# Coarse attention of two steps together on eight array tiles, with TensorE's order written out

## The chip, the cores and the metric

The kernel runs on one core of a Trainium2 chip (trn2). The metric is device time in microseconds (us) of one execution, the median over runs. TensorE is written PE, VectorE DVE, ScalarE ACT, GpSimd POOL, and SP is the engine that starts most transfers.

## The reference

Eight batches of eight heads, 576 positions, head dimension 64. Each head has two attentions, summed; a gated convolution over the 512 channels of a batch follows.

```
q_d, k_d, v_d = means of q, k, v over 4 neighbours        # 144 coarse positions
out_d   = softmax(scale * q_d @ k_d.T) @ v_d               # coarse attention
out_up  = repeat(out_d, 4)
scores  = where(|i - j| < 4, scale * q @ k.T, -1e9)        # local attention
x       = out_up + softmax(scores) @ v                     # then heads to channels
gate    = sigmoid(sum over 5 taps of conv_w[k] * x shifted by k)
out     = (gate * (x @ w_val)) @ w_out                     # float32 throughout
```

## The kernel before

A step is two pairs of heads of a batch, four heads; there are 16 steps (`NSTEP`), two to a batch. The kernel records each piece of work as an operation with its engine, a duration, what it needs and what it must wait for (`op`), and a planner (`Planner`) then plays all operations through and writes each engine's instructions in the order that comes out. PE's order is the one that the planner is given as a list: `tensor_order` makes it from `FIRST`, `PACE` and `TURN`. `SHIFT` moves due times, which decide among ready operations on DVE, ACT and POOL. For some operations the planner also picks the engine (`either`). Nothing is reordered on the chip: each engine runs its list and waits.

A step i has these operations. `sla`, `slb` (line 722): local scores in two halves, 24 matmuls each and 4 that add the band mask. `mx`, `sub`, `exp`, `sum`, `rcp`, `norm`, `turn`, `spr`: their softmax, a 32x32-block transpose on DVE and four copies. `sd` (line 811): coarse scores, 20 matmuls of 144 columns, five for each of four q (q is a head of the step); the result stands on 32 partitions for each q. Each coarse matmul of steps 4 to 15 reads 64 rows and fills 32 columns of the array (a 64x32 tile; steps 0 to 3 sum over 128 rows); the four q's lie on four of its eight such tiles. `cmx0`, `cbi`, `cexp`, `cgrd`, `crcp`, `cnorm`, `cturn`: the coarse softmax, with one buffer `pd` for the probabilities and one, `pdt`, for their transpose. `odp` (line 932): coarse values, 20 matmuls on tiles of 32 rows and 64 columns, again four of eight. `oc` (line 945): ACT copies them to `od`. `xa`, `xb` (line 888): local values in two halves of 24 matmuls on 64x64 tiles, written into free columns of the PSUM tiles that `odp` opened. `xu`, `xt` (line 903): DVE adds local and repeated coarse values into `xt`, in four instructions of 288 columns.

The convolution of a pair p: `xh`, `xl` split `xt` into two fp32r parts (POOL, ACT or DVE), `tap4` and four `tap`s on DVE (line 994) form the gate's argument in a buffer `gp`, ACT applies tanh. A block j of 504 (at the end 288) positions runs through two projections: `v` (val, lines 1096 to 1098: three fp32r matmuls for each of four channel chunks), `h` on DVE (gate times value), its split `hhi`, `hlo`, then `o` (out, the same three lines) and its copy and store. In PE's list, `p` counts such matmul groups.

PSUM has eight banks: three tiles of two banks under the tag "a" (`AB`), shared by local scores, coarse scores and the values of a step, and two tiles of one bank for the projections. Before, `odp` takes two of the three "a" tiles and they come free with the step's last `xt`. In the first stretch some matmuls on constants (line 579) keep PE busy.

SP starts the loads of `qk` (two for each pair), `vw` (local values), the first quarter of `qs` and `vs` (batches' four-neighbour sums, whose other three quarters POOL adds by accumulating transfers, line 606), the weights and the stores. The planner allows eight SP transfers at a time (`OUTSTANDING`).

## Time and profile before

| | us |
|---|---|
| median of 3 runs (367.65 to 465.03) | 369.12 |
| profiled execution | 368.75 |
| its span, first to last instruction | 367.0 |
| PE busy / DVE busy / ACT busy / POOL busy | 341.5 / 309.0 / 208.3 / 158.2 |
| share of PE in the chain that ended last | 62% |

One run of the three, 465.03, stands far from the other two. The span is what the trace shows; 1.75 us of the execution lie outside it. Busy time on PE counts overlapping matmuls once, and a matmul's end is modelled, so the distance from one start to the next says more than a duration. A float32 matmul appears as two records. "Idle before, <- X" names what ended a wait.

### The profile page before, as it was taken

How to read it: one execution, taken by the hardware profiler on the slowest of the kernel's cores; microseconds unless marked ns; L12 is line 12 of the kernel's file. 1: busy time of each engine (PE TensorE's matmuls, PEld its weight loads, DVE VectorE, ACT ScalarE, POOL GpSimd, SP SyncE). 2: the span in 40 equal slices, each digit the busy share in tenths (PEclk: the TensorE clock that was granted, in tenths of full speed). 3: DMA queues.
4: the chain of work that ended last, by engine and by line, in shares of the span. 5: the costliest groups of instructions: out<-in, count | busy, mean ns of one | idle time of the engine just before them, and what ended most of it. 6: DMA issues, size and time to landing. Idle time of an engine off the chain costs nothing.

```text
span 367.0 us, 12798 instructions
## 1 busy us (share of the span) xinstructions
PE 341.5 (93%) x5500; PEld 268.2 (73%) x5500; DVE 309.0 (84%) x487; ACT 208.3 (57%) x530; POOL 158.2 (43%) x170
## 2 busy tenths in 40 slices
PE   8669669699999999999999999999799999999996
PEld 5546447577787777777777777777577778788996
DVE  4699989999899999999999998999988993836720
ACT  1388556746676865587555756675376465314421
POOL 6878732955504644434453245633582323001100
PEclk9998889899999999999999999999999999999999
DMA  7999499899897799887989997969523301102012
GB/s 229 352 362 349 113 292 293 226 199 178 272 305 173 234 267 293 234 210 223 293 205 224 274 248 195 220 183 308 140 49 113 116 3 63 51 2 86 28 50 80
DMA packets 23464, 70.95 MB, mean 193 GB/s; under 512 B 3184, under 2 KB 9584, under 8 KB 23408
## 3 DMA queue, kind: packets, MB, share of 16 engines
q1 hardware_dynamic: 17504, 52.39, 41.0%
q0 software_dynamic: 5616, 17.50, 26.5%
q8 instruction: 43, 0.70, 0.7%
q10 hardware_dynamic: 288, 0.26, 0.2%
q14 instruction: 13, 0.11, 0.1%
HBM read 60.69 MB, written 9.44 MB: 191 GB/s over the span
## 4 chain that ended last, share of the span: by engine, by line
PE 62%; DVE 20%; ACT 7%; DMA 4%; issue 3%; SPq 1%; POOL 1%; ACTq 0%; POOLq 0%; DVEq 0%
PE out L1096 8%; PE val L1096 7%; PE out L1097 7%; PE out L1098 7%; DVE gp L994 7%; PE val L1098 6%; PE val L1097 6%; PE x L888 6%; PE x L932 4%; DMA qk<-in_qk 4%; PE sd L811 4%; PE sl L722 2%; DVE xt L903 2%; ACT pd L855 2%; ACT pt L574 2%
## 5 line engine op out<-in xcount | busy, mean ns | idle before, releaser
L994 DVE SCALAR_TENSOR_TENSOR gp<-xt,cw,gp 128x576 f32<-128x576 f32 x128 | 111.4, 902 | 1.3 <-ACT gp L979 0.6
L1096 PE MATMUL val<-xhs,wh_v 128*128 128x504 f32 (+1 forms) x160 | 64.0, 400 | 0.0
L1098 PE MATMUL val<-xls,wh_v 128*128 128x504 f32 (+1 forms) x160 | 60.3, 377 | 0.3 <-POOL xls L969 0.3
L1097 PE MATMUL val<-xhs,wl_v 128*128 128x504 f32 (+1 forms) x160 | 60.0, 375 | 0.0
L1096 PE MATMUL out<-hhl,wh_o 128*128 128x504 f32 (+1 forms) x144 | 58.6, 407 | 0.5 <-DVE h L1124 0.4
L1098 PE MATMUL out<-hhl,wh_o 128*128 128x504 f32 (+1 forms) x144 | 54.7, 380 | 0.0
L1097 PE MATMUL out<-hhl,wl_o 128*128 128x504 f32 (+1 forms) x144 | 54.6, 379 | 0.0
L1005 ACT ACTIVATE gp<-gp 128x576 f32<-128x576 f32 x32 | 21.9, 685 | 28.1 <-DVE gp L994 27.9
L1186 ACT ACTIVATE ob<-out 128x504 f32<-128x504 f32 (+2 forms) x40 | 21.8, 554 | 27.8 <-PE out L1098 24.0
L888 PEld LDWEIGHTS x<-pt,vw 64*64 64x64 f32 x1536 | 26.4, 138 | 14.6 <-issue 6.4
L903 DVE TENSOR_TENSOR xt<-x,od 128x288 f32<-128x288 f32 x64 | 26.0, 441 | 13.0 <-PE x L888 13.0
L1096 PEld LDWEIGHTS val<-xhs,wh_v 128*128 128x128 f32 x160 | 30.3, 190 | 8.5 <-issue 2.9
L1144 POOL TENSOR_TENSOR hhl<-h,hhl 128x504 fp32r<-128x504 f32 (+2 forms) x24 | 26.8, 1148 | 19.7 <-ACT hhl L574 19.1
L1098 PEld LDWEIGHTS val<-xls,wh_v 128*128 128x128 f32 x160 | 30.4, 190 | 5.9 <-POOL xls L969 0.7
L1096 PEld LDWEIGHTS out<-hhl,wh_o 128*128 128x128 f32 x144 | 27.0, 188 | 9.0 <-issue 3.3
L574 POOL COPY pt<-pt 32x576 f32<-32x576 f32 x23 | 16.9, 733 | 38.6 <-PE x L888 29.7
L1097 PEld LDWEIGHTS val<-xhs,wl_v 128*128 128x128 f32 x160 | 30.4, 190 | 4.1
L888 PE MATMUL x<-pt,vw 64*64 64x48 f32 x1536 | 30.1, 225 | 3.3 <-DVE xt L903 2.4
L606 POOL DMA_DIRECT2D vs<-in_vgr x21 | 20.3, 968 | 29.0 <-DMA vs<-in_vgr 20.8
L855 ACT ACTIVATE pd<-pd,crs 128x144 f32<-128x144 f32 x75 | 24.6, 405 | 12.3 <-DVE crs L849 12.2
L722 PE MATMUL sl<-qk 128*24 128x60 f32 x1536 | 26.8, 215 | 4.7 <-issue 2.0
L831 ACT ACTIVATE pd<-sd,cbi 128x144 f32<-128x144 f32 x80 | 29.9, 386 | 2.1 <-DVE h L1124 1.6
(94 smaller groups left out, 675.8 us busy)
## 6 DMA issues: line engine op xcount, KB each, us to landing
qk<-in_qk SPq DMA_DIRECT2D x64, 291.0 KB, 7.3
vw<-in_vw SPq DMA_DIRECT2D x16, 768.0 KB, 6.0
qs<-in_qkr POOLq DMA_DIRECT2D x18, 576.0 KB, 8.2
out_t<-ob SPq DMA_DIRECT2D x32, 252.0 KB, 4.6
vs<-in_vgr POOLq DMA_DIRECT2D x21, 320.0 KB, 7.5
qs<-in_qkr SPq DMA_DIRECT2D x6, 576.0 KB, 10.5
vs<-in_vgr SPq DMA_DIRECT2D x7, 320.0 KB, 7.2
raw_v<-in_w_val SPq DMA_DIRECT2D x4, 512.0 KB, 8.2
```

The lines of the kernel that those rows point to most:

```text
L574: (nc.scalar.copy if eng is nc.scalar else eng.tensor_copy)(out=to, in_=of)
L722: nc.tensor.matmul(out=sc[32 * q : 32 * q + BQ, 2 * KW * g : 2 * KW * (g + 1)].rearrange("p (h k) -> p h k", h=2), lhsT=t[:, 1, 3 + blk : ...
L831: nc.scalar.activation(out=pd[:, g, 0:SD], in_=s["cs"][:, g], func=AF.Exp, scale=1.0 / 128.0, bias=s["bi"][:, g : g + 1], accum_out=s["csm ...
L855: nc.scalar.mul(w[:, g], w[:, g], s["crs"][:, g : g + 1])
L888: nc.tensor.matmul(out=s["x", pr][r, part, 0:HALF].rearrange("p (e g j) -> p e g j", e=2, j=BQ)[:, :, g], lhsT=s["vw"][(LO, HI)[pr], n + h ...
L903: nc.vector.tensor_tensor(out=xt, in0=s["x", pr][:, part, 0:HALF].rearrange("p (e j r) -> p e j r", e=2, r=FAC), in1=od.broadcast_to([P, 2 ...
L994: nc.vector.scalar_tensor_tensor(out=s["gp"], in0=s["xt"][:, k : k + S], scalar=cw[:, c, k : k + 1], in1=s["gp"], op0=ALU.mult, op1=ALU.add,)
L1005: nc.scalar.activation(out=s["gp"], in_=s["gp"], func=AF.Tanh, scale=0.5)
L1096: nc.tensor.matmul(out=o, lhsT=wh[:, d, col], rhs=his[d], start=d == 0, stop=False)
L1097: nc.tensor.matmul(out=o, lhsT=wl[:, d, col], rhs=his[d], start=False, stop=False)
L1098: nc.tensor.matmul(out=o, lhsT=wh[:, d, col], rhs=los[d], start=False, stop=d == NC - 1)
L1144: eng.tensor_tensor(out=t["hl"][:, cs], in0=t["h"][:, cs], in1=t["hh"][:, cs].bitcast(F32), op=ALU.subtract)
```

## The change

From step 4 on, the two steps of a batch are computed together in the coarse attention. One call of `sd` computes the first three of five groups of queries for both steps (24 matmuls), a second call the other two (16); one call of `odp` computes the values of both steps (40 matmuls), two PSUM tiles, one for each step. In the odd step the two heads of a pair are exchanged (`^ n % 2`, and the host lays out `vg` accordingly), so that both steps' matmuls lie on different tiles of the array. The probabilities and their transposes share three buffers (`pds`); guard and reciprocal run once for a pair of steps. `xa` and `xb` each have a PSUM tile of their own, freed by one DVE add over both pairs (576 columns); the coarse values are copied by one ACT instruction for a step and their tiles are then free. There are two double `xt` buffers instead of four single ones and six `gp` buffers instead of seven.

PE's order is one list (`FIRST`), without `PACE`, `HOLD` and `TURN`. `SHIFT` grows from 17 to some 700 words. SP starts a transfer only when at most 3,000,000 bytes were started after the last one known to have landed (`FLIGHT`; `paced`, and a dependency between the two transfers). The planner's own costs for code loading change, which alters no instruction by itself. The first loads are put in a slightly different order (`EARLY`).

```diff
-GB = 7
+GB = 6
...
-PACE = ((2, 10), (4, 29), (14, 189))
-HOLD = 6
 OPENING, SWITCH = 33000, 200
...
-TURN = (("sla slb", 1, 3), ("sd", 1, 3), ("odp", 0, 3), ("xa", 0, 3), ("xb", 0, 4))
-    "l0 sd0 l1 sd1 odp0 x0 p2 odp1 p4 l2 p2 x1 sd2 p2"
+    "sla0 sd0 sd1 sla1 xb0 slb0 xa0 slb1 odp0 p4 odp1 p1 xb1 xa1 p3 sla2 sd2 sd3 sla3 odp2 p8 xa2 xb2 sd4 p7 odp3 xa3 sd5 xb3 sla4 slb2 p9 slb4 odp4 xa4 "
...
-CODE, FETCH, BEAR = 256, 5500, 300
+CODE, FETCH, BEAR = 256, 2700, 300
+FLIGHT = 3000000
...
+        def paced(now):
+
+            kept, left = [], FLIGHT
+            for x in reversed(sent):
+                left -= ops[x]["size"]
+                if left < 0:
+                    if x not in end or end[x] > now:
+                        return False
+                    kept = [x]
+                    break
+            self.behind = kept
...
-    pd = cpool.tile([P, NG, 32 * NB], F32, name="pd")
+    pds = [cpool.tile([P, NG * 32 * NB], F32, name=f"pd{i}") for i in range(3)]
-    xts = [cpool.tile([P, 4 + S], F32, name=f"xt{i}") for i in range(4)]
+    xts = [cpool.tile([P, 2, 4 + S], F32, name=f"xt{i}") for i in range(2)]
...
+    turns = [(n, i) for i in range(2 * SUMB) for n in ("pd", "pdt")]
+    turns += [(n, 2 * b + c) for b in range(SUMB, B) for n in ("pd", "pdt") for c in range(2)]
+
+    def probs(n, i):
+        return pds[turns.index((n, i)) % 3].rearrange("p (g k) -> p g k", g=NG)
+
+    def freed(n, i):
+
+        at = turns.index((n, i)) - 3
+        if at < 0:
+            return None
+        n, i = turns[at]
...
+        mate = [i] if i < 2 * SUMB else [i // 2 * 2, i // 2 * 2 + 1]
+        groups = range(NG) if i < 2 * SUMB else (range(3), range(3, NG))[i % 2]
+        main = mate[0]
...
+            for g in groups:
                 for q in range(4):
-                    p = 2 * i + q // 2
-                    if i < 2 * SUMB:
-                        rows, t = slice(0, P), st[p]["qs"]
-                        left, k = SD, t[:, 2 * SD * (q % 2) : 2 * SD * (q % 2) + SD]
-                    else:
-                        rows, t = (LO, HI)[q % 2], bt[i // 2]["qs"][:, p % NC].rearrange("p a j -> p (a j)")
-                        left, k = 0, t[:, SD : 2 * SD]
-                    nc.tensor.matmul(
-                        out=s["cs"][32 * q : 32 * q + 32, g],
-                        lhsT=t[rows, left + CQ * g : left + CQ * g + 32],
-                        rhs=k[rows],
-                        start=True,
-                        stop=True,
-                    )
+                    for n in mate:
+                        p, hd = 2 * n + q // 2, q % 2 ^ n % 2
+                        if i < 2 * SUMB:
+                            rows, t = slice(0, P), st[p]["qs"]
+                            left, k = SD, t[:, 2 * SD * hd : 2 * SD * hd + SD]
+                        else:
+                            rows, t = (LO, HI)[hd], bt[i // 2]["qs"][:, p % NC].rearrange("p a j -> p (a j)")
+                            left, k = 0, t[:, SD : 2 * SD]
+                        nc.tensor.matmul(
+                            out=place(n, g)[32 * q : 32 * q + 32],
+                            lhsT=t[rows, left + CQ * g : left + CQ * g + 32],
+                            rhs=k[rows],
+                            start=True,
+                            stop=True,
+                        )
 
...
+        op(("sd", i), "PE", 1330 if x == NG else 36 * 4 * x, mm, pooled, banks=[("a", exps)],
+           cols=(2880 if i < 2 * SUMB else 288 * x, WARM), code=80 if x == NG else 16 * x)
...
+        if i == main:
+            every = exps if i < 2 * SUMB else [(f"cexp{x}", i) for x in range(6)] + [(f"cexp{x}", i + 1) for x in range(4)]
+            op(("cgrd", i), "DVE", 80, guard, every, port=ALONE)
...
+        op(("cnorm", i), either(820, 1700, 1550), 0, norm, [("crcp", main)], port=BOTH)
+        op(("cturn", i), "DVE", 890, turn, [("cnorm", i)], free=[freed("pdt", i)])
...
-                keep_warm(s["x", 0][:, part])
+                s["x", part] = ps.tile([P, 2, 512], F32, tag="a", name=f"x{part}_{i}", bufs=AB)
+                keep_warm(s["x", part][:, 0])
-                                out=s["x", pr][r, part, 0:HALF].rearrange("p (e g j) -> p e g j", e=2, j=BQ)[:, :, g],
+                                out=s["x", part][r, pr, 0:HALF].rearrange("p (e g j) -> p e g j", e=2, j=BQ)[:, :, g],
...
-        op(("xa", i), "PE", 810, mm(0), [("vw", i), ("odp", i), ("oc0", i), ("oc1", i)] + spreads(i), cols=(1150, WARM), code=96)
-        op(("xb", i), "PE", 810, mm(1), [("xa", i)], cols=(1150, WARM), code=96)
+            op((x, i), "PE", 810, mm(part), [("vw", i), values(i)] + spreads(i), banks=[("a", [(k, i)])], cols=(1150, WARM), code=96)
+                (k, i), "DVE", 790, combine(part), [(x, i), ("oc", i)],
...
+            for n in mate:
+                at[n]["y"] = ps.tile([P, 2, 512], F32, tag="a", name=f"y{n}", bufs=AB)
+            keep_warm(s["y"][:, 0])
+                    for n in mate:
+                        h = q % 2 ^ n % 2
+                        nc.tensor.matmul(
+                            out=at[n]["y"][64 * h : 64 * h + 64, q // 2, 0 : NG * CQ].rearrange("p (g j) -> p g j", j=CQ),
+                            lhsT=u["vs"][32 * q : 32 * q + 32, NB * (n % 2) + b],
+                            rhs=at[n]["pdt"][32 * q : 32 * q + 32, :, b, 0:CQ],
+                            start=b == 0,
+                            stop=b == NB - 1,
+                        )
+
+        def evac(n):
...
-            ("odp", i), "PE", 1360, mm, [("vb", i) if i < 2 else ("vs3", i // 2), ("cturn", i)],
-            banks=[("a", [(f"xu{pr}", i), (f"xt{pr}", i)]) for pr in range(2)], cols=(1450, WARM), code=80,
+                ("odp", i), "PE", 1360 + 90 * (len(mate) - 1), mm,
+                [("vb", i) if i < 2 else ("vs3", i // 2)] + [("cturn", n) for n in mate],
+                banks=[("a", [("oc", n)]) for n in mate], cols=(1450 * len(mate), WARM), code=80 * len(mate),
...
+        op(("oc", i), "ACT", 390, evac(i), [values(i)], free=[("xt", i - 2)])
...
+    vg = np.stack([vg[:, 0], vg[:, 1, :, ::-1]], axis=1)
...
```

The names that follow are the program's, with running numbers; a number behind "x" joins equal rows. On PE, about step 6, before, around a coarse score call (`sd`), which stands inside a run of value projections:

```order
L1098 MATMUL val_0_1998<-xls,wh_v 128x504
L811 MATMUL sd_2049<-qs_978 32x144 x20
L1096 MATMUL val_0_1998<-xhs,wh_v 128x504
L1097 MATMUL val_0_1998<-xhs,wl_v 128x504
L1098 MATMUL val_0_1998<-xls,wh_v 128x504
```

The same place in the changed order, the pair of steps 6 and 7:

```order
L1205 MATMUL val_2_1577<-xls,wh_v 128x504
L900 MATMUL sd_1588<-qs_813 32x144 x24
L996 MATMUL x_4_1616<-pt_76,vw_1066 64x2x24 x24
L777 LDWEIGHTS ident_b
L777 MATMUL sl_1648<-mask_b,ident_b 32x360
```

The call has 24 matmuls for two steps, and a half of local values and one of local scores follow it without a projection between. The second call of the pair, with 16, stands later.

The coarse values (`odp`) on PE before, for step 6:

```order
L1097 MATMUL val_1_2079<-xhs,wl_v 128x504
L1098 MATMUL val_1_2079<-xls,wh_v 128x504
L932 MATMUL x_6_2096<-pdt_1963,vs_1295 64x145 x2
L932 MATMUL x_6_2097<-pdt_1963,vs_1295 64x145 x2
L932 MATMUL x_6_2096<-pdt_1963,vs_1295 64x145 x2
```

And in the changed order, for steps 6 and 7:

```order
L1204 MATMUL out_3_1937<-hhl_1_1643,wl_o 128x504
L1205 MATMUL out_3_1937<-hhl_1_1643,wh_o 128x504
L1042 MATMUL y_1949<-pd_79,vs_1266 64x145
L1042 MATMUL y_1950<-pd_77,vs_1266 64x145
L1042 MATMUL y_1949<-pd_79,vs_1266 64x145
```

Before, ten such rows of two make up a step; now forty rows alternate between the two steps' PSUM tiles, and the call stands between output projections of block 1.

On DVE, the adds into `xt` before, at step 4 and 5:

```order
L903 TENSOR_TENSOR xt_82<-x_4_1611,od_4_1640 128x2x144
L903 TENSOR_TENSOR xt_83<-x_4_1612,od_4_1646 128x2x144
L749 TENSOR_TENSOR ex<-sl_1536,mx_1661 128x24x30
L861 STREAM_TRANSPOSE pdt_1753<-pd 128x800
L903 TENSOR_TENSOR xt_83<-x_4_1612,od_4_1646 128x2x144
```

In the changed order:

```order
L1010 TENSOR_TENSOR xt_84<-x_4_1616,od_1564 128x2x2x144
L810 TENSOR_REDUCE mx_1796<-sl_1648 128x24
L1251 TENSOR_TENSOR hhl_3_1791<-h_3_1778,hhl_3_1791 128x252
L815 TENSOR_TENSOR ex<-sl_1648,mx_1796 128x24x30
L917 TENSOR_REDUCE cmx_1841<-sd_1721 128x4
L1010 TENSOR_TENSOR xt_85<-x_5_1813,od_1566 128x2x2x144
```

One instruction now covers both pairs of a half step, and it reads the PSUM tile that only this half uses.

## Rows read from the trace of the kernel before

**Rows 1.** The page: busy us, share of the span and instructions of each engine

```profile
PE 341.5 (93%) x5500; PEld 268.2 (73%) x5500; DVE 309.0 (84%) x487; ACT 208.3 (57%) x530; POOL 158.2 (43%) x170
```

**Rows 2.** Stretches (us): length, busy us by engine, granted clock, DMA share, GB/s

```profile
0.00:80.00 80.00, 62.04 (x1197) 45.79 (x1197) 68.66 (x90) 45.54 (x116) 50.68 (x59) 0.91 0.87 268
80.00:300.00 220.00, 215.75 (x3739) 166.43 (x3738) 208.74 (x344) 139.57 (x368) 98.84 (x102) 1.00 0.78 210
100.00:260.00 160.00, 158.30 (x2787) 121.67 (x2785) 153.45 (x252) 102.46 (x279) 71.16 (x77) 1.00 0.89 239
300.00:333.00 33.00, 33.00 (x353) 26.45 (x352) 16.91 (x29) 12.18 (x24) 5.25 (x7) 1.00 0.10 37
```

**Rows 3.** Waits of PE, 82 us to the end: us in total, times, longest

```profile
PE x L888 <- DVE xt L903: 2.4, 1, 2.4
PE x L888 <- ACT od L945: 0.9, 2, 0.7
PE out L1096 <- DVE h L1124: 0.4, 1, 0.4
PE sd L811 <- PE out L1098: 0.3, 1, 0.3
```

**Rows 4.** PE in order of time: start us, us, instruction, records (137 to 146)

```profile
137.21 0.39 PE L1098 MATMUL val<-xls,wh_v 128*128 128x504 f32 x1
137.53 1.43 PE L811 MATMUL sd<-qs 64*32 64x144 f32 x40
138.89 0.50 PE L1096 MATMUL val<-xhs,wh_v 128*128 128x504 f32 x1
139.23 0.39 PE L1097 MATMUL val<-xhs,wl_v 128*128 128x504 f32 x1
139.46 0.39 PE L1098 MATMUL val<-xls,wh_v 128*128 128x504 f32 x1
...
141.15 1.46 PE L932 MATMUL x<-pdt,vs 32*64 32x145 f32 x40
142.54 0.50 PE L1096 MATMUL val<-xhs,wh_v 128*128 128x504 f32 x1
...
144.79 0.92 PE L888 MATMUL x<-pt,vw 64*64 64x48 f32 x48
145.64 0.50 PE L1096 MATMUL val<-xhs,wh_v 128*128 128x504 f32 x1
```

**Rows 5.** The chain that ended last: start us, us, piece (local scores)

```profile
170.78 0.63 PE sl L722 x48
```

**Rows 6.** DVE by line: count, busy us, mean ns, idle; then two places in time

```profile
L994 DVE SCALAR_TENSOR_TENSOR gp<-xt,cw,gp 128x576 f32<-128x576 f32 x128 | 111.4, 902 | 1.3 <-ACT gp L979 0.6 <-POOL gp L981 0.4
L903 DVE TENSOR_TENSOR xt<-x,od 128x288 f32<-128x288 f32 x64 | 26.0, 441 | 13.0 <-PE x L888 13.0
L969 DVE TENSOR_TENSOR xls<-xt,xhs 128x576 fp32r<-128x576 f32 x17 | 13.5, 810 | 2.2 <-ACT xhs L574 1.7 <-POOL xhs L574 0.5
L843 DVE TENSOR_SCALAR cs<-csm 128x5 f32<-128x5 f32 x16 | 4.0, 250 | 0.0
L849 DVE RECIPROCAL crs<-cs 128x5 f32<-128x5 f32 x16 | 2.8, 172 | 0.0
...
254.01 2.59 DVE L994 SCALAR_TENSOR_TENSOR gp<-xt,cw,gp 128x576 f32<-128x576 f32 x2
...
273.50 5.10 DVE L994 SCALAR_TENSOR_TENSOR gp<-xt,cw,gp 128x576 f32<-128x576 f32 x7
```

**Rows 7.** PE in order of time: the last local values and the last matmul

```profile
331.69 0.92 PE L888 MATMUL x<-pt,vw 64*64 64x48 f32 x48
...
363.40 0.30 PE L1098 MATMUL out<-xls,wh_o 128*128 128x288 f32 x1
```

**Rows 8.** PE in order of time: coarse values of step 1, in the opening

```profile
35.89 1.20 PE L932 MATMUL x<-pdt,vs 32*64 32x145 f32 x29
40.26 0.71 PE L932 MATMUL x<-pdt,vs 32*64 32x145 f32 x11 [3.17 <-issue]
```

More of the change, by code (lines that the diff above doesn't have):

```diff
@@ L136, in add, with backlog @@
         self.queue[q].append([t + self.FIRST[q], float(size), key])
+    def backlog(self, t):
+        left = sum(max(0.0, x[1]) for l in self.queue.values() for x in l) / 1e3 / self.ALONE["SP"]
+        return max(0.0, left - max(0.0, t - self.now))
     def rates(self):
@@ L469, in emit @@
             self.warm = self.idle.get(k, 0)
-            o["fn"](*([self.engines[self.who[k]]] if o["pick"] else []))
+            self.sent[k] = o["fn"](*([self.engines[self.who[k]]] if o["pick"] else []))
+            for x in self.pace.get(k, ()):
+                self.after(self.sent[k], self.sent[x])
 def tensor_order():
@@ L585, in keep_warm, with after @@
             )
-    plan = Planner({"DVE": nc.vector, "POOL": nc.gpsimd, "ACT": nc.scalar})
+    def after(late, early):
+        tc.add_manual_dep(
+            late.ins,
+            early.ins.name,
+            mybir.DependencyInfo(mybir.DependencyClass.Sync, mybir.DependencyReason.DATA),
+            reason="transfers under way",
+        )
+    plan = Planner({"DVE": nc.vector, "POOL": nc.gpsimd, "ACT": nc.scalar}, after)
     op = plan.op
@@ L873, in coarse_scores @@
-        op(("crcp", i), "DVE", 110, recip, [("cgrd", i)])
-        op(("cnorm", i), either(820, 1700, 1550), 0, norm, [("crcp", i)], port=BOTH)
-        op(("cturn", i), "DVE", 890, turn, [("cnorm", i)], free=[("odp", i - 1)])
+            to, of = turns.index(("pdt", i)) % 3, turns.index(("pd", i)) % 3
+            s["pdt"] = pds[to].rearrange("p (g b k) -> p g b k", g=NG, k=32)
+            nc.vector.transpose(out=pds[to], in_=pds[of])
+        exps = [(f"cexp{x}", i) for x in range(len(mate) * len(groups))]
```

216 lines of the change are left out of this document (103 added, 113 removed), and 52 rows, old and new, of tables (FIRST, SHIFT).

## Prediction

> **What bounds the kernel now.** I read the busy shares and slices first, then the stretches, then TensorE's waits, then TensorE instruction by instruction. The reader should see three engines of very different kinds of fullness. TensorE (PE) is busy 93% of the span and VectorE (DVE) 84% [rows 1]; neither number says which one sets the end, because the kernel has stages. By stretches [rows 2]: in the first 80 us PE is busy 62.0 of 80 and the mean granted clock is 0.91, while DVE does 68.7 and the DMA engines are 0.87 busy; this opening is paced by loads and by DVE. From 80 to 300 us PE is busy 215.8 of 220 at clock 1.00, and from 300 to 333 it is busy without a break. After 82 us PE waits for another engine for 2.4 us once and 0.9 us in two pieces, little more in all [rows 3]. So from 80 us to the end PE is the bound: each microsecond of work taken from it there shortens the run, as long as nobody else becomes late. DVE is the one to watch: 153.5 busy of the 160 us between 100 and 260, 95.9% [rows 2], and it only gets idle after 300, 16.9 busy of 33, where PE still works off projections without a break. Only there has DVE time to spare.
>
> What PE does in the saturated part is readable from starts alone [rows 4]. A wide projection matmul (504 columns) follows the one before after 0.23 us. A step's coarse scores (20 matmuls, 40 records) take 1.36 us from their start to the next start, 137.53 to 138.89; its coarse values take 1.39, 141.15 to 142.54. Each interruption of a projection run also costs beside its own time: the last wide matmul before it takes 0.32 instead of 0.23 (137.21 to 137.53), the first one after it 0.34 (138.89 to 139.23). That is 0.20 for each run of projections.
>
> **The change, part by part.** *Scores (sd), steps 4 to 15.* Before, the four q's of a step use four 64x32 tiles of the array, five matmuls on each: 1.36/5 = 0.27 us per matmul and tile. After, two steps stand together and the exchanged heads of the odd step put its matmuls on the other four tiles: 40 matmuls in two calls of 24 and 16, again five per tile. If eight tiles run side by side as four do now, a pair costs 3 x 0.27 + 2 x 0.27 plus two fills, about 0.90 + 0.62 = 1.52. If no more than four run at a time it costs 2.72 as now. A third limit is how fast PE takes records: the local values pass 48 of them in 0.85 us (144.79 to the next start, 145.64 by the same view), 17.5 ns each [rows 4], and the local scores 48 in 0.63, 13 ns each [rows 5]; 80 records need 1.05 to 1.40, below 1.52. The nearest rows favour 1.52: every tile form in the trace already runs its tiles side by side. Saved: 6 x (2.72 - 1.52) = 7.2 us.
>
> *Values (odp).* The same with eight 32x64 tiles: two steps in one call of 40 matmuls, five per tile. One step takes 1.39 now; 80 records at 17.5 ns take 1.40; I take 1.45, the other end is 2.78. Saved: 6 x (2.78 - 1.45) = 8.0 us.
>
> Here a rule of the Trainium skill speaks against the change. The records above follow each other at 17.5 and 13 ns [rows 4, 5]. The page "TensorE: Matmul & The Clock Gate" (section "Wait — 56ns, not 53.3ns?") says that start-to-start never drops below about 25 ns however few columns a matmul has; by that the 80 records of a pair would need 2.0 us in either product, and the two terms would be 4.3 and 4.7 us instead of 7.2 and 8.0, as an estimate from that page. The trace does not agree for these narrow tiles, so the sum keeps the rows.
>
> *Fewer interruptions.* In the listed order of PE from the first output product on there are 66 runs of projections before and 41 after. At 0.20 that is 5.0 us; I take 0.18, 4.5 us, since small products that now follow each other change the array's shape between them too. The changed order also leaves half a step's local scores for after that point: 0.63 us [rows 5] and its mask matmuls, +0.9 as an estimate. Sum on PE: 7.2 + 8.0 + 4.5 - 0.9 = 18.8 us.
>
> *Banks.* Local values get PSUM tiles of their own, freed by the add that reads them, and the coarse values are freed as soon as ACT has copied them. Before, both tiles of a step stayed held from the coarse values to the last of four adds; that is the 2.4 us wait for xt in [rows 3]. I credit nothing for it: a full DVE can be late elsewhere.
>
> *DVE.* The 64 half-width adds become 32 of double width. They hold 26.0 us now; 32 at the 0.81 of a 576-wide instruction [rows 6] are 25.9: no gain. The six spared guard and reciprocal pairs save 6 x (0.25 + 0.17) = 2.5. By the listed order ten two-input instructions go from DVE to GpSimd (six xl, three norm, one hlo) and five come back; 5 x 0.81 = 4.0 saved. But GpSimd then does more beside DVE, and that has a price: seven taps in a row take 5.10 us, 0.73 each, in one place, and two take 2.59 in another, where GpSimd works at the same time; the mean over all 128 is 0.90 [rows 6]. Ten more such meetings cost from 0 to 0.57 x 10 = 5.7; I take 3. Net: 3.5 us less.
>
> *Does DVE keep up?* The last local values start at 331.7 now and PE ends at 363.7 [rows 7]. In the changed order 21 more wide matmuls (4.8 us) stand behind that product, so with 18.8 us saved it would start at 331.7 - 18.8 - 4.8 = 308.1. DVE has done 68.7 + 208.7 + 16.9 = 294.3 us of work by 333 [rows 2]; less 3.5 it needs 290.8 by about 309, which is 222.1 in the 229 us after the opening, 97%. It has shown 95.9%. At that pace it needs 231.6: 2.6 us late, and PE waits for it.
>
> *Loads.* SP now also waits until an earlier transfer has landed when over 3 MB are under way; loads and result stores queue behind that wait. In the saturated part no wait of PE ends with a transfer [rows 3], and the order of the first loads barely moves. I price it at nothing; the cover is the two-step buffers, and without it a load's landing of some 7 us would show once per step.
>
> *Opening.* DVE's list up to the gated product of the last unit of block 0 holds nearly the same work in both kernels, so I leave its end at 80 us.
>
> Span: 367.0 - 18.8 + 2.6 = 350.8. The profiled execution took 368.75 in all, 1.75 beyond its span, and the median of the runs is 369.12, 0.1% away. Forecast: 352.6, rounded to **353 us**.
>
> **Rivals.** *DVE becomes the bound.* For it: 95.9% busy already, and GpSimd's load grows. If every one of the ten meetings costs its 0.57 and DVE holds only the 94.9% of 80 to 300 [rows 2], it needs 225/0.949 = 237 us, 8 us late: 348.2 + 8 + 1.75 = 358. Against: waits of DVE for others are small now, and the adds no longer wait for four instructions. Chance 0.16.
>
> *Records slow down in eight-tile streams.* Midway between the 17.5 ns of the local values and the 34 of today's scores (1.36 over 40 records [rows 4]) lie 26 ns, 2.06 us for a pair in either product; the terms become 4.0 and 4.3, 6.9 us less: 359.5. For it: nothing here has run eight tiles. Against: 17.5 and 13 ns [rows 4, 5]. Chance 0.05. This is about what the rule of the Trainium skill's page "TensorE: Matmul & The Clock Gate", given above, would make of it; the trace so far disagrees with it.
>
> *The change does not do what it says:* eight tiles run no more side by side than four, the first two terms vanish: 367.0 - 3.6 + 1.75 = 365, no change. Against: shapes with four column tiles and with two by two tiles both run side by side. Chance 0.08.
>
> *Slower: PE runs out of instructions.* In the opening the coarse values of a step stop in the middle of their own matmuls for 3.17 us with nothing to wait for but issue [rows 8], while the DMA engines are 0.87 busy [rows 2]. The denser calls take instructions twice as fast, between loads as dense (0.89 from 100 to 260). There are 18 such calls (12 of scores, 6 of values). Six stops of 3.17 eat the 18.8; from eight on the kernel is over 2% slower; ten give 367 + 13 + 1.75 = 382. Against: after 82 us no such stop shows in PE's waits [rows 3]. Chance 0.05.
>
> **How the numbers follow.** The forecast's case has 0.66 and by itself spans 347 (no DVE loss, and the 3.3 us of waits of [rows 3] gone too) to 358. The range 347 to 362 adds the DVE and the record cases and leaves out about 0.2. Two per cent, what a measurement of this kernel can tell from no change, is 7.4 us: under 361.7 is faster. That holds for the forecast, the record case and nearly all of the DVE case: 0.83. The no-gain case and the rim of the others give 0.12, slower 0.05.
>
> **What would show it.** Right: paired values near 1.45 us and the two score calls near 0.90 and 0.62 from start to next start; some 41 runs of projections; PE without waits from about 80 us; the last local values near 308 to 312. Wrong: 2.0 or 2.7 us for the pairs; waits of PE ending with DVE over 5 us after 82; "issue" stops inside the paired calls; DVE's mean tap above 0.95; an opening that ends later than 80 us.

## The result, and the profile after

The changed kernel takes 357.39 us, the median of four runs (354.56 to 361.41), against 369.24 before: a ratio of 0.967, 95% interval 0.9626 to 0.9715. It is faster, inside the range, and 4.4 us above the forecast. The traced execution is the longest of the four, 361.41 with a span of 359.6, so every account below ends 4 us above the median one. It counts as a slow run (over 1.5% above the fastest of the four), and a second trace of the same kernel (first experiment, span 358.0), which does not, is set beside it where the two differ.

The page after, in the columns of [rows 1], and two of the stretches, in those of [rows 2]:

```profile
PE 325.8 (91%) x5490; PEld 257.2 (72%) x5490; DVE 297.4 (83%) x438; ACT 209.1 (58%) x511; POOL 160.7 (45%) x170
```

```profile
80.00:300.00 220.00, 208.06 (x3888) 162.06 (x3887) 202.20 (x301) 140.10 (x355) 107.34 (x111) 0.98 0.74 200
100.00:260.00 160.00, 149.06 (x2885) 115.68 (x2884) 145.31 (x216) 98.54 (x254) 80.39 (x83) 0.98 0.85 226
```

PE is busy 15.7 us less, DVE 11.6 less. But in the stretch where PE was saturated it is now idle for 11 of 160 us, and DVE fell from 95.9% to 90.8%: the engine that was the bound and the one that threatened to become it both stand still more. Waits of PE from 82 us on, in the columns of [rows 3], say for what:

```profile
PE x L996 <- issue: 3.0, 2, 2.0
PE sd L900 <- issue: 2.5, 2, 1.4
PE out L1203 <- DVE h L1231: 2.3, 2, 2.0
PE sl L788 <- issue: 1.9, 2, 1.0
PE x L996 <- POOL pt L632: 1.6, 1, 1.6
PE val L1203 <- ACT ob L1293: 0.3, 1, 0.3
```

"issue" was in no row of [rows 3]. Now it is the largest releaser, 7.4 us in six stops. The stops lie in the dense parts. PE in order of time, start and duration first; a call of coarse values, and 5 us later the first of a pair's two calls of coarse scores:

```profile
100.86 1.54 PE L1042 MATMUL y<-pd,vs 32*64 32x145 f32 x80
102.33 0.92 PE L996 MATMUL x<-pt,vw 64*64 64x48 f32 x48
...
106.11 0.71 PE L900 MATMUL sd<-qs 64*32 64x144 f32 x30
108.21 0.67 PE L900 MATMUL sd<-qs 64*32 64x144 f32 x18 [1.38 <-issue]
108.81 0.91 PE L996 MATMUL x<-pt,vw 64*64 64x48 f32 x48
```

80 records of coarse values take 1.47 us from start to the next start, as forecast. The scores stop after 30 of their 48 records with nothing to wait for, and go on 1.66 us after the start of the last of them. The DMA queues (packets, MB, share of 16 engines) show what this view doesn't. First 103.0 to 105.5 us, where no q8 is among them, then 105.5 to 108.5:

```profile
q1 hardware_dynamic: 192, 0.73, 94.0%
```

```profile
...
q8 instruction: 1, 0.02, 2.0%
```

q8 carries PE's program, 43 packets of 16 KB (0.70 MB) in the whole run, one for each 256 of PE's some 11,000 records. Counting PE's records (matmuls, weight loads and the sequencer's waits together) through the trace puts all six stops after 82 us on one place in a block, and sets each beside the packet that started last before it:

```
record   its number mod 256   packet starts   PE goes on   from packet to PE   time lost
 3521           193              105.83         108.21           2.38            1.64
 4801           193              137.41         139.81           2.40            1.16
 6081           193              173.22         176.02           2.80            1.36
 6593           193              186.24         188.67           2.43            1.17
 6849           193              197.28         199.65           2.37            2.24
10177           193              291.60         294.17           2.57            1.13
```

(Records are numbered from the first one that the trace has; that the edges of the blocks lie at 193 and not at 0 is put down to records ahead of it. "Time lost" is the distance to the next start less what it takes without a stop. The packet at 173.22 itself took 1.44 us. A seventh pause of 0.33 at 278.6 stands on no such record.) In the other traces of this case, whatever the order of PE's list, every "issue" wait of PE of 0.3 us or more after 82 us stands on a record with 193 modulo 256 as well, and PE goes on 2.2 to 2.6 us after a packet's start (3.6 in one case).

The stop at 106.8 us reads: the block begun at record 3265 was entered at about 101.5; the packet for the next one started only at 105.83, after the load queue had kept the engines 94% busy; the block was used up at 106.8; PE went on 2.38 us after the packet's start.

### The profile page after: what moved, and what is told of

Same layout as the page of the kernel before. It is cut to its first block, busy times and chain, and to the rows that moved or that the text cites. A ratio compares the mean times of both kernels' runs of the same rounds, so it can differ in the third digit from the quotient of the medians.

```text
span 359.6 us, 12689 instructions
## 1 busy us (share of the span) xinstructions
PE 325.8 (91%) x5490; PEld 257.2 (72%) x5490; DVE 297.4 (83%) x438; ACT 209.1 (58%) x511; POOL 160.7 (45%) x170
## 4 chain that ended last, share of the span: by engine, by line
PE 61%; DVE 14%; DMA 12%; POOL 5%; issue 3%; ACT 3%; SPq 1%; POOLq 0%; ACTq 0%; DVEq 0%
PE out L1203 9%; PE out L1205 8%; PE out L1204 8%; PE val L1203 8%; DVE gp L1101 7%; PE val L1205 7%; PE val L1204 7%; PE x L996 5%; DMA raw_o<-in_w_out 4%; PE y L1042 3%; PE sl L788 3%; PE sd L900 2%; DMA out_t<-ob 2%; DMA raw_v<-in_w_val 2%; DMA vw<-in_vw 2%
## 5 line engine op out<-in xcount | busy, mean ns | idle before, releaser
L1101 DVE SCALAR_TENSOR_TENSOR gp<-xt,cw,gp 128x576 f32<-128x576 f32 x128 | 104.0, 856 | 0.1
L1203 PE MATMUL val<-xhs,wh_v 128*128 128x504 f32 (+1 forms) x160 | 62.3, 389 | 1.0 <-DVE h L1231 0.6
L1203 PE MATMUL out<-hhl,wh_o 128*128 128x504 f32 (+1 forms) x144 | 59.1, 410 | 3.3 <-DVE h L1231 3.1
L1205 PE MATMUL out<-hhl,wh_o 128*128 128x504 f32 (+1 forms) x144 | 56.5, 392 | 0.1
L1204 PE MATMUL out<-hhl,wl_o 128*128 128x504 f32 (+1 forms) x144 | 56.4, 392 | 0.0
L1231 DVE SCALAR_TENSOR_TENSOR h<-gp,val 128x288 f32<-128x288 f32 (+6 forms) x64 | 26.3, 445 | 13.7 <-PE val L1205 12.3
L1251 POOL TENSOR_TENSOR hhl<-h,hhl 128x504 fp32r<-128x504 f32 (+1 forms) x25 | 26.2, 1060 | 23.9 <-ACT hhl L632 14.1
L1203 PEld LDWEIGHTS out<-hhl,wh_o 128*128 128x128 f32 x144 | 27.9, 194 | 11.9 <-issue 4.0
L632 ACT COPY pt<-pt 32x576 f32<-32x576 f32 x46 | 30.8, 670 | 9.1 <-DVE pt L838 7.5
L1205 PEld LDWEIGHTS out<-hhl,wh_o 128*128 128x128 f32 x144 | 27.9, 194 | 6.4 <-POOL hhl L1251 0.5
L1204 PEld LDWEIGHTS out<-hhl,wl_o 128*128 128x128 f32 x144 | 27.9, 194 | 4.7
L672 POOL DMA_DIRECT2D vs<-in_vgr x21 | 18.4, 906 | 28.2 <-DMA vs<-in_vgr 16.2
```

What stands on the lines that cost most here:

```text
L632: (nc.scalar.copy if eng is nc.scalar else eng.tensor_copy)(out=to, in_=of)
L672: nc.gpsimd.dma_start(out=u[nm], in_=src[b, r], accum_op=ALU.add)
L1101: nc.vector.scalar_tensor_tensor(out=s["gp"], in0=s["xt"][:, k : k + S], scalar=cw[:, c, k : k + 1], in1=s["gp"], op0=ALU.mult, op1=ALU.add,)
L1203: nc.tensor.matmul(out=o, lhsT=wh[:, d, col], rhs=his[d], start=d == 0, stop=False)
L1204: nc.tensor.matmul(out=o, lhsT=wl[:, d, col], rhs=his[d], start=False, stop=False)
L1205: nc.tensor.matmul(out=o, lhsT=wh[:, d, col], rhs=los[d], start=False, stop=d == NC - 1)
```

## Experiments

The theory tested, **late code**: PE's work fell as forecast, and what is missing was lost because the denser calls use up 256 records faster than the next packet arrives. The rivals: DVE (or another engine's list) would have held PE back anyway; or the pacing of loads or the tile exchange itself costs something.

**1. The changed kernel once more.** No edit; the runs of the next three are measured beside it.

> The changed kernel once more, nothing altered. Theory (late code): PE's code arrives in blocks of 256 instruction records, and where PE has run through a block before the next one has landed it stops with nothing to wait for; in the traced execution after the change seven such stops of 0.3 to 2.2 us, 9.0 us in all, stand at multiples of about 256 records after 100 us, and granted clock lost behind them is another 2 to 3 us. By this theory the stops stand again at the same record numbers (some come, some go, since they hang on the traffic of the moment), 4 to 9 us in all, and the time is 354 to 361. Rival (the traced execution was an odd one): hardly any stop, all times within 1 us of 355.

Measured 357.77, ratio 0.9708 (0.965 to 0.9766). Its trace (span 358.0) has stops on five of the six records of the table (not on 6849), 8.3 us in all against 8.7, but with other lengths: the one at 6593 lasts 3.33 instead of 1.17. The place belongs to the program; the length changes from one execution to the next.

**2. Four tiles instead of eight.** The exchange of heads is taken out, the paired calls and everything else stay.

```diff
-                        p, hd = 2 * n + q // 2, q % 2 ^ n % 2
+                        p, hd = 2 * n + q // 2, q % 2
...
-                        h = q % 2 ^ n % 2
+                        h = q % 2
...
-    vg = np.stack([vg[:, 0], vg[:, 1, :, ::-1]], axis=1)
```

> The changed kernel without the exchange of heads in the odd step (the values of v are laid out accordingly): the matmuls of both steps fall on the same four tiles; every engine's order stays as it is. This prices the eight tiles by themselves. A pair's two score calls take 2.7 us instead of 1.57 and the pair's values 2.8 instead of 1.47, six times each, 7 + 8 = 15 us more on PE. Theory (late code: stops come from calls that run through a block of 256 records too fast): the slower calls give the stops back, 4 to 9 us, so 362 to 368. Rival 1 (stops have nothing to do with density): 357.4 + 15 = 372. Rival 2 (the tiles were never what gained): 356 to 359.

Measured 365.87, ratio 0.9943 (0.9914 to 0.9973). The same calls in PE's order of time:

```profile
99.90 2.86 PE L1042 MATMUL y<-pd,vs 32*64 32x145 f32 x80
102.69 0.92 PE L996 MATMUL x<-pt,vw 64*64 64x48 f32 x48
...
106.48 1.73 PE L900 MATMUL sd<-qs 64*32 64x144 f32 x48
108.14 0.92 PE L996 MATMUL x<-pt,vw 64*64 64x48 f32 x48
```

In the changed kernel the first score call, where no stop cuts it, reads:

```profile
135.12 0.99 PE L900 MATMUL sd<-qs 64*32 64x144 f32 x48
136.04 0.50 PE L1203 MATMUL val<-xhs,wh_v 128*128 128x504 f32 x1
```

2.79 for a pair's values against 1.47; 1.66 for its first score call against 0.92, and for the second, read in the same way, 1.15 against 0.65. So eight tiles run side by side and are worth 6 x 1.32 + 6 x 1.24 = 15.4 us on PE's own path. The time grew by 8.1 us only. Where the rest went shows in this kernel's waits of PE after 82 us:

```profile
PE sl L788 <- issue: 2.4, 2, 1.5
...
PE x L996 <- issue: 0.9, 1, 0.9
```

With the slower calls the stops at 3521, 4801 and 6081 are gone, and 3.9 us of time lost to stops are left where the changed kernel has 8.3. The granted clock does not fall either, from 80 to 300 us in the columns of [rows 2]:

```profile
80.00:300.00 220.00, 213.20 (x3864) 170.50 (x3864) 197.54 (x295) 136.78 (x348) 101.56 (x106) 1.00 0.73 197
```

Of the 15.4 - 8.1 = 7.3 us that did not arrive, these 4.4 us of stops and the clock, 0.98 in the changed kernel (2% of 220 us are another 4.4, an estimate), are enough to make up the whole: PE's gain was paid back as waiting for code and as a slower clock. How much of each can't be said, since experiments 6 and 9 show that a stop taken away is not worth its length.

**3. Fewer bytes moved.** From the ninth pair on, `qk` loads bring 64 of 582 columns, and from the fifth step on `vw` loads a twelfth; the old contents of the tiles are used, so the output is not the reference's. Instructions stay the same.

```diff
+                w = KS if p < 2 * QB else 64
-                return nc.sync.dma_start(out=s["qk"][hd::2, hd : hd + 2], in_=qk[b, c][(LO, HI)[hd]])
+                return nc.sync.dma_start(out=s["qk"][hd::2, hd : hd + 2, 0:w], in_=qk[b, c][(LO, HI)[hd]][:, :, 0:w])
...
+            w = 2 * NI if p // 2 < 2 * WB else 2
-            return nc.sync.dma_start(out=u["vw"], in_=vw[p // 2])
+            return nc.sync.dma_start(out=u["vw"][:, 0:w], in_=vw[p // 2][:, 0:w])
```

> The changed kernel with most bytes of two loads left out: from the ninth pair on a qk transfer brings 64 of 582 columns, from the fifth step on a vw transfer brings a twelfth, so the local attention of later steps is computed on old data. The same instructions in the same order on every engine, some 22 MB of 71 less moved. Theory (late code: the block's transfer stands behind data transfers): the stops after 100 us go, the clock is 1.00, 9 + 3 us are gained less what was small in the other executions: 345 to 351. Rival (a block takes its time whatever else is moved, dense calls alone outrun it): the stops stay, 355 to 359.

Measured 350.45, ratio 0.9518 (0.9485 to 0.955), 7.3 us less than the changed kernel beside it. The stretch from 100 to 260 and the waits of PE after 82 us:

```profile
100.00:260.00 160.00, 153.12 (x3009) 119.74 (x3002) 152.05 (x228) 105.42 (x271) 85.29 (x89) 0.99 0.60 128
```

```profile
PE sl L791 <- issue: 3.1, 2, 2.3
...
PE sd L903 <- issue: 1.4, 1, 1.4
```

The DMA share falls from 0.85 to 0.60, and the stops at 3521, 4801 and 6849 are gone; those at 6081, 6593 and 10177 stay. So traffic makes half of the stops: their packets started 195 to 239 records into the running block. The packets of the other three started 77 to 116 records into it, little later than where the DMA engines are idle (51 to 99, last section), so there the density of the calls is what is left to explain them; quite without traffic stands only the one at 10177 (DMA share 0.03 from 291 to 294 us). Both PE (95.7%) and DVE (95.0%) are fuller than in the changed kernel (93.2% and 90.8%). The gain is more than the 3.2 us by which the stops shrank. Between the two traces (358.0 and 349.4) another 1.2 us lie in the opening, which ends at 75.81 instead of 76.97. From there to 340 us the granted clock stands at its lower level for 3.4 us instead of 10.2, worth 3.4 us if half of that time is lost (an estimate), and PE's waits for other engines fall from 3.9 to 3.1. So this run does not price the stops alone.

**4. Loads not paced.** The two lines that tie a transfer to an earlier landing are left out.

```diff
-            for x in self.pace.get(k, ()):
-                self.after(self.sent[k], self.sent[x])
```

> The changed kernel without the added waits of SP (at most 3 MB under way): the same order, some seven waits of transfers for transfers gone. Theory (late code): where more data is queued a block arrives later, so stops of the same number or a few more, 356 to 361. Rival (the waits cost: loads come late): 353 to 355. Priced at nothing in the prediction: 357.

Measured 356.71, ratio 0.9694 (0.9651 to 0.9737), the same as the changed kernel, and the same six stops. Pacing at 3 MB costs nothing and brings nothing. The trace shows one thing more: its stops are as long (8.1 us in PE's waits, 7.2 in experiment 1), yet its span is 354.6, since the granted clock does not fall behind them:

```profile
80.00:300.00 220.00, 208.10 (x3899) 162.06 (x3898) 205.87 (x305) 141.44 (x355) 105.91 (x108) 1.00 0.73 200
```

**5. Fewer bytes in the kernel before.** The edit of experiment 3 in the kernel before.

> The kernel before the change with the same bytes left out as in the light run of the changed kernel (from the ninth pair on 64 of 582 columns of qk, from the fifth step on a twelfth of vw; the local attention of later steps is computed on old data); the same order on every engine. Theory (late code): after 82 us the kernel before has no stop for code, so fewer bytes give it next to nothing: 366 to 369. Rival (fewer bytes speed up every kernel by less contention): 361 or less, as the changed kernel went from 357.8 to 350.5.

Measured 367.61, ratio 0.9974 (0.9953 to 0.9995). Loads cost the kernel before nothing that can be seen; without them the changed one is 7 us faster. What made them matter is the change.

**6. Projections moved between the dense calls.** 23 of PE's projection pieces are moved in its list to stand between dense calls (nothing else moves, and the work is the same). `v3.2:3>sla:10` reads: piece v3.2 of pair 3 goes behind `sla` of step 10.

```diff
+SPREAD = "v2.2:1>v2.1:1 v2.3:1>v2.2:1 v3.0:1>xb:4 v3.1:1>v3.0:1 v3.2:1>v3.1:1 v1.1:2>v1.0:2 v1.2:2>v1.1:2 v1.0:3>sla:9 v1.1:3>v1.0:3 v1.2:3>slb:9 v1.3:3>v1.2:3 v2.0:3>v1.3:3 v3.2:3>sla:10 v3.3:3>v3.2:3 o0.0:3>sd:11 ..."
```

> The changed kernel with 23 projection pieces (three matmuls each) moved a few places on PE alone, so that they stand between the dense calls in whose blocks of 256 records PE stopped: two before the first score call of steps 6 and 7, three between local values and local scores of steps 4 and 6, two before the local values of step 6, seven around the calls of steps 9 and 10, seven in steps 10, 9 and 14, two before step 14's scores. Every other engine keeps its order; PE has five more runs of projections, 5 x 0.2 = 1 us. Theory (late code: PE reads a block faster than the next can land): where the last 192 records of a block take 3 us or more of work, hardly a stop stays; of some 9 us of stops after 100 us 1 to 3 stay, and the time is 349 to 353 beside 357 of the changed kernel. Rival (the stops are only slack that DVE would take anyway): the stops go, waits for DVE come in their place, 355 to 358.

Measured 359.59, ratio 0.9722 (0.9676 to 0.9768): no gain. Waits of PE after 82 us, and then PE's stretches (length, PE busy, granted clock, DMA share, GB/s):

```profile
PE out L1249 <- DVE h L1277: 7.9, 3, 3.8
...
PE sl L823 <- issue: 0.5, 1, 0.5
```

```profile
188.00:192.00 4.00, 2.51 (x6) 0.60 0.99 264
192.00:196.00 4.00, 4.00 (x59) 0.54 0.24 34
```

The stops went as the theory says (to 0.5), and the time did not. PE now waits 7.9 us for DVE's gated product, and the clock falls behind that wait as it does behind a stop. I read it so: with projections done earlier, the next ones in PE's list come up sooner, and these need a product that DVE makes no earlier.

**7. Both: moved projections and fewer bytes** (edits of 6 and 3).

> The moved projection pieces and the bytes left out together (local attention of later steps on old data). Theory (late code): both take away the same stops, so the second gives little more: 346 to 350; what is left then is the prediction's own sum with its waits. Rival (two different causes): the gains add, 342 to 345.

Measured 355.75, ratio 0.9651 (0.9593 to 0.971): 5.3 us slower than fewer bytes alone. Its stops are gone, and PE waits 7.3 us for DVE's product after 82 us. The moved pieces cost more than they bring in stops.

**8. The due times of before.** `SHIFT` with its 17 words of before in the changed kernel: PE's list stays the same, the lists of DVE, ACT and POOL and some choices of engine change (DVE 452 instructions, ACT 494, POOL 161).

> The changed kernel with the 17 words of SHIFT of the kernel before in place of some 700: other orders on DVE, ACT and GpSimd, PE's calls and their pairs as in the changed kernel. The prediction took the list for what moved between engines alone. If the gain is PE's (shorter pairs, fewer runs), the kernel keeps most of it: 357 to 363. If it hung on the orders of the other engines (rival), it goes back to 365 or more, with waits of PE for DVE, ACT or GpSimd in place of the gain.

Measured 372.30, ratio 1.0094 (1.0068 to 1.012). Waits of PE from 55 to 345 us:

```profile
PE out L1156 <- DVE h L1184: 7.6, 4, 4.1
PE sl L741 <- issue: 7.4, 6, 2.7
PE val L1156 <- DVE h L1184: 5.0, 3, 2.5
```

The saved matmuls bring nothing when the other engines' lists are not planned for the new order: 12.6 us of waits for DVE, whose busy time (309.2) is that of before, and more stops for code on top. Which of these makes how much of the 14 us between it and the changed kernel was not told apart.

**9 and 10. Fewer pieces moved.** 14 pieces, seven of them put between the dense calls of steps 9 and 10 (the words with `:3>`, but for the two that begin with o2); then the other seven alone.

```diff
+SPREAD = (
+    "v2.2:1>v2.1:1 v1.1:2>v1.0:2 v1.2:2>v1.1:2 v0.2:3>sla:9 v0.3:3>v0.2:3 v1.0:3>slb:9 v1.1:3>v1.0:3 v1.2:3>v1.1:3 v3.2:3>sla:10 v3.3:3>v3.2:3 "
+    "o2.0:3>o1.3:3 o2.1:3>o2.0:3 v3.2:6>xb:14 v3.3:6>v3.2:6"
+)
```

> The changed kernel with 14 projection pieces moved on PE alone, differently from the first such kernel: one before step 6's scores, two before step 6's local values, two between the two local value halves of step 9, two after step 14's local values; and around steps 9 and 10 the dense calls come earlier instead of later: step 9's local scores directly behind one block's end, two pieces behind the first half, three behind the second, and two between step 10's local scores and step 11's coarse scores. Other engines keep their order. Theory (late code, with DVE nearly as full as PE: a dense call that comes later makes DVE wait, so pieces may only stand where PE stopped anyway or behind calls that come earlier): most stops go and DVE's waits do not grow, 351 to 355. Rival (any gain on PE is eaten by the wait for DVE): 356 to 359.

> The same without the moves around steps 9 and 10: seven pieces, four places. Theory (late code, DVE nearly as full): the stops in step 6's scores, step 6's local values, step 9's local values and step 15's local scores go (1.0 to 1.6, 1.2 to 1.6, 0 to 2.2 and 0.7 to 1.1 us in the traces so far), those in the scores of step 10 and the local scores of step 10 stay: 353 to 356. Rival (eaten by the wait for DVE): 356 to 359.

Measured 356.09 over six runs, ratio 0.9665 (0.9638 to 0.9691), and 357.62 over six, 0.9733 (0.9703 to 0.9762). Waits of PE after 82 us with 14 pieces:

```profile
PE out L1248 <- DVE h L1276: 5.3, 2, 2.9
...
PE val L1250 <- issue: 0.6, 1, 0.6
```

The stops in this view went from 7.4 to 0.6 us, the waits for DVE from 2.3 to 5.3, and the median by 1.3 to 1.7 us: its interval overlaps that of the changed kernel. With seven pieces nearly half of the stops stay (3.2 us), PE waits 3.2 us for DVE, and nothing is gained. The version with 14 is the fastest one here that computes the whole reference, but not clearly faster than the changed kernel.

**11. Less work on DVE.** One of the five taps works on 64 of 576 columns from the ninth pair on, so the gate is not the reference's. DVE's busy time falls by 14.2 us (297.2 in the trace of experiment 1), to 283.0; PE's list is that of the changed kernel.

```diff
+                w = 64 if k == 1 and p >= 8 else S
```

> The changed kernel with one of the five taps of the gate on 64 of 576 columns from the ninth pair on (the rest of that tap is left out): the same instructions in the same order, 24 x some 0.65 = 16 us less work on DVE, PE's work and its traffic as before. Theory (two lists that hold each other up: PE stops for code and then DVE, full and in order, makes PE wait as well): the waits for DVE go, 4 to 5 us, the stops for code stay: 351 to 354. Rival 1 (PE alone bounds, its waits for DVE are made by its own stops): 356 to 358. Rival 2 (DVE alone bounds): the 16 us come off, 343 or less.

Measured 353.89 (352.15 to 358.88), ratio 0.959 (0.9531 to 0.965). **12. Both**, less on DVE and the 14 moved pieces:

> The 14 moved pieces (which alone gave 356.1 beside 357.4 to 357.8) and the short taps together (one tap of five on 64 of 576 columns from the ninth pair on). Theory (two lists that hold each other up): with DVE ahead, taking away the stops for code is worth its full length, some 7 us beyond the short taps alone: 344 to 347. Rival (the moved pieces gain little for another reason, as lost clock or more runs of projections): within 2 us of the short taps alone, 350 to 353.

Measured 353.55, ratio 0.957 (0.953 to 0.9609). Waits of PE after 82 us, first with the short tap, then with both:

```profile
PE sl L788 <- issue: 2.2, 2, 1.5
PE sd L900 <- issue: 2.1, 2, 1.8
PE x L996 <- issue: 2.1, 2, 1.1
...
PE out L1204 <- DVE h L1232: 0.8, 1, 0.8
```

```profile
PE val L1249 <- ACT ob L1339: 3.3, 2, 2.8
PE out L1249 <- DVE h L1277: 1.6, 2, 1.4
```

A DVE with time to spare takes some 4 us off, though the stops stay at 6.4. That DVE's fullness costs this much by itself isn't shown, for the granted clock differs as well. With the short tap it reads 1.00 from 80 to 300 us, where both traces of the changed kernel have 0.98:

```profile
80.00:300.00 220.00, 211.13 (x3954) 164.89 (x3936) 194.72 (x308) 143.36 (x358) 104.90 (x108) 1.00 0.74 201
```

PE's waits for other engines, what a faster DVE shortens directly, fell by 1.5 us only (3.9 in experiment 1, 2.4 here). With the stops gone as well (none is left) nothing more is won: PE then waits 2.8 us for ACT's copy of an output block at 204 us. Up to 203 us this kernel had gained some 4 us on the one before it, counted from the end of the opening; it gave them back there.

What these twelve settle: the stops exist, where they lie, what starts them and that traffic lengthens them. That removing them is worth their length is refuted, in three ways (6, 9, 12): each time another in-order list stood next in line, and the clock fell behind the new waits (0.98, 0.98 and 0.99 from 80 to 300 us). What the stops cost the changed kernel, net, stays open: between the 1.7 us at most of experiment 9 and the 7.3 of experiment 3, in which the opening and the clock gained too. No run holds the clock still, so it remains a rival for part of the differences between experiments 3, 4, 9 and 11.

## Why the prediction was right, and where it was 4 us off

**Scores, values, fewer interruptions: right.** A pair's values take 1.47 (1.45 forecast), its two score calls 0.92 and 0.65 (0.90 and 0.62), and there are 41 runs of projections. From the end of the opening to the end of the span, PE's own work, waits and stops and slower clock taken out, went from 281.8 us to 263.4: 18.4 saved, 18.8 forecast. Experiment 2 shows that it is the eight tiles that do it. The rule weighed there, 25 ns from start to start (the Trainium skill, "TensorE: Matmul & The Clock Gate", section "Wait — 56ns, not 53.3ns?"), does not hold here: 80 records follow each other in 1.47 us, 18 ns each. The rival of slower records and the one of no change are out.

**Instruction supply: the step that failed.** The rival was put on the far side only, with a 3.17 us stop and "after 82 us no such stop shows in PE's waits" against it. What happened is that rival in a smaller size: six stops with 1.45 us each on average, 9.0 with the small pause. The absence of stops before was read as supply enough. The trace of before, counted in blocks of 256 records, shows otherwise: its four shortest blocks after 82 us take 3.46 to 4.18 us, and in three of them the next packet starts 2.40 to 2.47 us ahead of need, just the 2.4 that PE needs after a packet's start. There was next to no margin; in the trace of experiment 5 the kernel before does stop once, 0.56 us on record 2753 (193 modulo 256). In the changed kernel the densest blocks would pass in 2.0 to 2.4 us without their stop. The stop of [rows 8], in the opening, was of this same kind: it stands on record 1217 of before (193 modulo 256) and ends 2.25 us after the start of a packet at 38.01; so was a second one there, 1.7 us on record 1729, which ends 2.40 us after a packet at 53.10.

**The clock behind a stop: not in the sum.** One stretch of PE after, and the same one before (length, PE busy, granted clock, DMA share, GB/s):

```profile
200.00:204.00 4.00, 4.00 (x16) 0.61 0.88 202
```

```profile
200.00:204.00 4.00, 4.00 (x59) 1.00 0.94 222
```

After the 2.24 us stop that ends at 199.65, 24 output matmuls take 7.13 us instead of 5.72, since for part of them the granted clock is at the lower of its two levels, 1.2 GHz:

```profile
201.11 0.62 PE L1205 MATMUL out<-hhl,wh_o 128*128 128x504 f32 x1
201.53 0.62 PE L1203 MATMUL out<-hhl,wh_o 128*128 128x504 f32 x1
```

0.42 from start to start, not the 0.23 of [rows 4]. The same after a wait of 1.8 for GpSimd's copy at 233 us (21 matmuls, 6.59 for some 5.1) and some 0.6 in smaller places: 3.5 us in all. It does not follow every stop: experiment 4, with the same six, shows none after the opening. Over the four executions of experiment 1 the mean granted clock was 0.965, 0.966, 0.975 and 0.981 at 359.81, 358.15, 357.39 and 355.11 us, so the spread between executions goes along with it.

**DVE: right in sign, too small.** 11.6 us less busy instead of 3.5. The taps got shorter, not longer, and the double-width adds did gain (after, in the columns of [rows 6]):

```profile
L1101 DVE SCALAR_TENSOR_TENSOR gp<-xt,cw,gp 128x576 f32<-128x576 f32 x128 | 104.0, 856 | 0.1
...
L1010 DVE TENSOR_TENSOR xt<-x,od 128x576 f32<-128x576 f32 x32 | 23.6, 744 | 5.1 <-PE x L996 4.9
```

The mean tap went from 0.902 to 0.856, and the taps' busy time fell by 7.4 where 3 us of extra meetings with GpSimd had been charged. Counted from the two traces, a tap that overlaps none of GpSimd's work takes 0.80 to 0.81 in both; 27 of the 128 overlap some of it before, with a mean of 1.27, and 21 after, with a mean of 1.11. Six of those before lie mostly beside GpSimd's addition that makes `hhl` and take 1.78 on average; after the change one does. So it matters with which of GpSimd's instructions a tap meets, and not only how many of them there are.

**Does DVE keep up: half right.** The forecast gave DVE 97% and 2.6 us of lateness. PE's waits for other engines after the opening, counted like the stops from start to start, are 5.0 us, hardly more than the 4.75 before, and 2.4 less than the forecast's 7.35 (4.75 kept and 2.6 added). But DVE did not run at 97%: it waits for PE. Waits of DVE from 80 to 300 us, before and after (us in total, times, longest):

```profile
DVE xt L903 <- PE x L888: 2.5, 4, 1.1
```

```profile
DVE h L1231 <- PE val L1205: 4.9, 6, 3.2
DVE xt L1010 <- PE x L996: 4.2, 4, 2.0
DVE cmx L917 <- PE sd L900: 3.0, 3, 1.5
DVE mx L810 <- PE sl L788: 2.9, 4, 1.2
```

15.0 us in place of 2.7 (with 0.2 in another row); 14.2 in the second trace, 11.6 without pacing and 10.1 with fewer bytes. I read it so: a stop of PE makes DVE late, and DVE, nearly full, can't catch up; its lateness comes back to PE as a wait for the next product. Experiments 6 and 9, where PE's waits for DVE grew as its stops went, fit this, but no run isolates one such exchange. By that reading neither engine alone is the bound from 80 us on: the two lists hold each other. The forecast's "each microsecond of work taken from it there shortens the run" was too simple, and experiments 6, 9, 11 and 12 are the measure of it.

**Banks, loads, opening.** The wait for `xt` is gone, no wait of PE after 82 us ends with a transfer, and pacing costs nothing (experiment 4): as priced. But the loads' cover was thinner than said, since they delay code. The opening's last wait ends at 78.69 instead of 80.45, 1.8 us to the good; in the second trace it ends at 76.97 and without pacing at 76.51, with the same work behind it. The prediction left this at nothing, and why it gains was not tested.

**The sum once more:** 350.8, + 0.4 (PE's work), + 9.0 (stops), + 3.5 (clock), - 2.4 (waits for others), - 1.8 (opening) = 359.5; the traced span is 359.6. PE's work (18.4) is what the other terms leave over of the span, so the sum closes by its making. That the median lies only 4.4 us from the forecast is in part luck: of the 16.2 us credited to the part behind the opening, 5.6 arrived in this trace and 5.5 in the second (286.5 us before; 280.9 and 281.0 after), and the opening, credited with nothing, gave 1.8 and 3.5. The last local values, due at 308 to 312, start at 318.99 (317.41 in the second trace), late by the stops and the clock.

## What to carry to other kernels

When PE's small matmuls are made denser, count its records (matmuls, weight loads and its sequencer's waits) in blocks of 256 and see what the change makes of the time of each: here blocks of 2.0 to 2.4 us stopped, one of them beside nearly idle DMA engines, and behind a full load queue blocks of 4.4, 5.0 and 8.7 us did. In a kernel with two engines above 90% in lists fixed beforehand, a stall taken out of one can be handed to the next list, as in experiments 6, 9 and 12, so price a change by the pair of them and plan the other lists again (the same matmuls with the due times of before were 0.9% slower than the kernel before). That a wait is absent from a trace bounds nothing until its margin is known.

## What was not expected of the hardware

PE's program streams in during the run: 16 KB packets of 256 records. PE goes on 2.37 to 2.43 us after a packet's start in four of the six stops (2.57 and 2.80 in the others). From 254 to 296 us, where the DMA engines are mostly idle (share 0.18), all seven packets start 51 to 99 records into the running block; in the loaded stretch from 90 to 200 us (0.93) nine of sixteen start 130 to 239 records into it. A page of the Trainium skill ("Runtime: NRT & Kernel Launch", section "Instruction fetch mechanics") says that PE's next 16 KiB are fetched while the current ones execute, and that this is hidden because instructions are issued more slowly than they arrive. The blocks and the fetching ahead agree with the trace; the hiding does not: six stops, 8.7 us.

In the second trace of the changed kernel, after the 3.33 us stop at 187.5 us, the granted clock shows 0.50 over a whole 4 us (length, PE busy, granted clock, DMA share, GB/s):

```profile
192.00:196.00 4.00, 4.00 (x11) 0.50 1.06 321
```

So the price of an idle PE can be more than the idle time: here the wide matmuls that follow take 0.42 instead of 0.23 for a while.
